# Chunk rows by broadcast copies, an early activation table, weights by need, and a first block in two 128-query parts

## The chip, the cores and the metric

One core of one Trainium2 chip. The metric is the device time of one execution in microseconds (us). One execution of each kernel is profiled: times inside a kernel come from its trace and count from the start of its span, which is about 2 us shorter than the timed run.

## The reference, cut to what matters

```python
# attention: 4 batches, 8 heads, 768 positions, head dim 64; chunks of 32 keys
k_min, k_max = min and max of every 32-key chunk
ub = sum_d max(q*k_min, q*k_max)                # upper bound of each chunk per query
ub = where(query chunk >= key chunk, ub, -1e9)
select the 6 chunks with the largest bound; mask the rest and the future
attn = softmax(q k^T / 8, masked) @ v
# FFN on the 3072 tokens of width 512
xn = x / rms(x) * rms_g
out = (silu(xn @ w_gate) * (xn @ w_val)) @ w_out   # d_ff 1536
```

A query among the first 192 has at most six chunks in its past, so it needs no bound: every past chunk is selected.

## The kernel before

The work is cut into 12 blocks of 256 queries (4 batches, 3 blocks each) and 24 jobs (a block and 4 of its 8 heads). For each job: k and q are loaded (`kraw`, `qraw`), transposed by VectorE (DVE) to `kT`, `qT`, cast to `kb`, `qb`; chunk minima and maxima go into `KS`; PE forms the bound `ub`; DVE turns and ranks it and makes a mask. Then scores `sc`, exponentials `pt`, values `avn`, normalised `xnat`. For each block follow `xs`, a turn by PE (`tp`), `xsT`, and the FFN: gate `gp`, value `vp`, hidden `hh`, output `op`.

The order of instructions on each engine is fixed in Python by a list scheduler: every operation has a planned duration, a priority (`key`, lower is sooner) and, for loads, a planned landing. An engine then works through its list in order; what stands at the head and waits holds everything behind it. Where PE's plan has a gap of over 0.5 us the kernel inserts matmuls on a zero tile ("idle matmuls"), meant to keep the clock up. Their number is fixed when the program is built; they run whether or not the gap is there on the chip.

```python
    warm(psF.tile([P, 512], FP32, name="wps", tag="bank")[:], 44)   # 44 idle matmuls first
    # ...
    def spread_rows(c0, c1, l0, l1, eng):      # the mask rows, from partitions 0-31 to the rest
        if eng == "SP":
            for a in range(1, 4):
                r = slice(32 * a, 32 * (a + 1))
                nc.sync.dma_start(out=late[r, l0:l1], in_=late[0:32, l0:l1])
                nc.sync.dma_start(out=chunkrow[r, c0:c1], in_=chunkrow[0:32, c0:c1])
            return
    # ...
    rows = add("SP", 2600.0, -3000.0, lambda e, w: spread_rows(BLK, S, BLK, S, "SP"), rows,
               lands=(300.0, 92.0))
    rm = add("SP", 430.0, SOON, lambda e, w: nc.sync.dma_start(
        out=rmsg[:], in_=moe_rms_g.rearrange("(g p) -> p g", p=P)), early=8000.0, lands=(100.0, 20.0))
    # ...
    key = blk_of(j) - 0.8 + 0.1 * g            # preparation of job j
    # ...
    key = blk + 3.1                            # FFN of block blk
```

The softmax here doesn't subtract the row's maximum and nothing guards it: scores larger than these inputs give would overflow.

## Time and profile before

Median 325.95 us.

| | us |
|---|---|
| span of the profiled execution | 324.1 |
| first real FFN matmul (gp) | 46.0 |
| PE idle plus idle matmuls before it | 32.1 |
| the same after it | 6.4 |
| k of job 4 reaches DVE | 29.9 |

The two rows of losses come from PE's timeline: I add the idle time in brackets, and for rows that read the zero tile the time until the next row begins. (The prediction's total, 37.2 us, leaves out the 1.25 us before the first matmul; it split that total as 31.5 and 5.7, where this count gives 32.1 and 6.4.) The page of the kernel before: busy time of each engine; then, in 40 slices of the span, the busy tenths of PE, its granted clock and the DMA engines' busy share.

```profile
PE 306.3 (95%) x4639; PEld 222.7 (69%) x4639; DVE 205.8 (64%) x525; ACT 225.0 (69%) x391; POOL 191.9 (59%) x332
...
PE   8977699989699999999999999999999999899995
...
PEclk9996999999799999999999999999999999999999
DMA  8999995465455442105453130100001001000001
```

PE looks full, but the first five slices (40 us) hold much that is not work. Its timeline (start us, duration us, what, and in brackets the idle time before and what ended it):

```profile
1.25 11.83 PE L263 MATMUL wps<-idle 128*128 128x512 bf16 x44 [1.25 <-DVE idle L258]
12.92 2.75 PE L263 MATMUL ub<-idle 128*128 128x512 bf16 x12
15.61 0.21 PE L421 MATMUL ub<-late,ident 64*64 64x32 bf16 x4
...
24.15 0.21 PE L421 MATMUL ub<-late,ident 64*64 64x128 bf16 x1 [1.19 <-DMA late<-late]
25.46 0.25 PE L421 MATMUL ub<-late,ident 64*64 64x128 bf16 x3 [1.10 <-DMA late<-late]
...
46.01 1.05 PE L649 MATMUL gp<-xsT,wg 128*128 128x256 bf16 x8
```

56 idle matmuls stand before the first bound at 15.6 us; PE then waits for spread rows; the FFN begins at 46 us. SyncE's timeline shows what stands before the loads of job 4:

```profile
15.80 0.40 SPq L751 DMA_DIRECT2D rmsg<-in_moe_rms_g_dram  x1
16.32 0.59 SPq L298 DMA_DIRECT2D late<-late  x1
...
20.60 4.54 SPq L233 DMA_DIRECT2D kraw<-in_k_dram  x4
```

The rms gain took 8.0 us to land, the rows about 7 us each.

### The profile page before, as it was taken

What the parts mean: (1) busy time and instruction counts of PE and PEld (TensorE: products, weight loads), DVE (VectorE), ACT (ScalarE), POOL (GpSimd) and SP (SyncE); (2) the same over time, 40 slices, a digit from 0 to 9 for tenths busy, and PEclk for the clock granted to TensorE, in tenths of its full rate; (3) what the DMA queues carried; (4) which work ended last, traced back from release to release, by engine and by line L of the source; (5) the groups of instructions that cost most, each with busy time, mean ns of one, the idle gap of its engine ahead of it and who ended that gap; (6) DMA issues with size and microseconds to landing.
All of it is one profiled execution on the core that took longest, in us unless ns stands there. A gap on an engine that the chain in (4) does not pass through costs nothing.

```text
span 324.1 us, 11419 instructions
## 1 busy us (share of the span) xinstructions
PE 306.3 (95%) x4639; PEld 222.7 (69%) x4639; DVE 205.8 (64%) x525; ACT 225.0 (69%) x391; POOL 191.9 (59%) x332
## 2 busy tenths in 40 slices
PE   8977699989699999999999999999999999899995
PEld 3434378658586787687685887785886876768682
DVE  7573989899499999159988577275466331523230
ACT  3251669786499998796778779766865986636461
POOL 8962538971896878297483567575452451635251
PEclk9996999999799999999999999999999999999999
DMA  8999995465455442105453130100001001000001
GB/s 170 203 213 237 225 164 145 123 167 163 137 144 132 145 121 68 67 2 132 132 136 96 51 85 16 53 2 35 34 3 37 31 3 67 0 34 32 34 32 66
DMA packets 43604, 30.30 MB, mean 93 GB/s; under 512 B 29536, under 2 KB 34336, under 8 KB 43552
## 3 DMA queue, kind: packets, MB, share of 16 engines
q1 hardware_dynamic: 34224, 23.81, 26.2%
q0 software_dynamic: 8944, 5.24, 11.4%
q8 instruction: 36, 0.59, 0.8%
q10 hardware_dynamic: 384, 0.52, 0.5%
q14 instruction: 16, 0.13, 0.1%
HBM read 28.31 MB, written 6.29 MB: 107 GB/s over the span
## 4 chain that ended last, share of the span: by engine, by line
PE 75%; DMA 8%; ACT 6%; DVE 5%; issue 2%; SPq 1%; POOL 1%; ACTq 0%; DVEq 0%; POOLq 0%
PE op L679 18%; PE gp L649 18%; PE vp L649 17%; PE avn L561 6%; DMA kraw<-in_k_dram 6%; PE sc L507 6%; PE ub L421 5%; ACT pt L531 3%; DMA rmsg<-in_moe_rms_g_dram 2%; PE sc L520 2%; PE tp L622 2%; SPq L233 1%; DVE kT L361 1%; ACT vs L661 1%; ACT th L657 1%
## 5 line engine op out<-in xcount | busy, mean ns | idle before, releaser
L672 POOL TENSOR_TENSOR hh<-tg,vs 128x512 bf16<-128x512 bf16 x72 | 83.5, 1160 | 54.2 <-ACT vs L661 44.9
L531 ACT ACTIVATE pt<-sc 128x768 bf16<-128x768 f32 (+1 forms) x96 | 84.1, 915 | 11.2 <-PE sc L520 10.9
L665 DVE SCALAR_TENSOR_TENSOR tg<-th,gp 128x512 bf16<-128x512 bf16 x72 | 49.0, 682 | 55.2 <-ACT th L657 53.8
L649 PE MATMUL vp<-xsT,wv 128*128 128x256 bf16 x576 | 75.4, 274 | 1.0 <-DVE tg L665 1.0
L649 PE MATMUL gp<-xsT,wg 128*128 128x256 bf16 x576 | 75.7, 275 | 0.0
L679 PE MATMUL op<-wo,hh 128*128 128x512 bf16 x288 | 65.2, 379 | 0.0
L649 PEld LDWEIGHTS <-wv 128*128 128x128 bf16 x576 | 54.8, 98 | 9.2 <-issue 1.5
L649 PEld LDWEIGHTS <-wg 128*128 128x128 bf16 x576 | 54.4, 98 | 8.4 <-issue 0.5
L661 ACT ACTIVATE vs<-vp 128x512 bf16<-128x512 f32 x72 | 43.3, 601 | 14.5 <-PE vp L649 10.8
L657 ACT ACTIVATE th<-gp 128x512 bf16<-128x512 f32 x72 | 43.3, 601 | 11.7 <-PE gp L649 11.6
L679 PEld LDWEIGHTS <-hh 128*128 128x128 bf16 x288 | 27.2, 98 | 30.7 <-POOL hh L672 0.3
L543 POOL TENSOR_SCALAR_AFFINE_SELECT pt<-pt 128x512 bf16<-128x512 bf16 x48 | 30.3, 643 | 23.9 <-ACT pt L531 23.1
L561 PE MATMUL avn<-VX,pt 128*128 128x65 bf16 x672 | 30.3, 195 | 5.3 <-POOL pt L543 2.8
L561 PEld LDWEIGHTS <-pt 128*128 128x128 bf16 x672 | 25.8, 98 | 11.1 <-POOL pt L543 3.1
L507 PE MATMUL sc<-qb,kb 32*128 32x256 bf16 (+1 forms) x768 | 32.4, 259 | 0.2 <-DVE ubn L431 0.2
L686 ACT ACTIVATE osb<-op 128x512 f32<-128x512 f32 x24 | 14.3, 597 | 24.8 <-PE op L679 24.8
L361 DVE STREAM_TRANSPOSE qT<-qraw 128x512 f32<-128x512 f32 x24 | 26.4, 1098 | 3.8 <-DMA qraw<-in_q_dram 3.7
L361 DVE STREAM_TRANSPOSE kT<-kraw 128x512 f32<-128x512 f32 x24 | 26.2, 1100 | 2.8 <-DMA kraw<-in_k_dram 2.7
L575 DVE RECIPROCAL rden<-avn 128x4 f32<-128x4 f32 x48 | 8.2, 172 | 26.1 <-PE avn L561 26.0
L520 PE MATMUL sc<-mt,chunkrow 32*128 32x128 bf16 (+1 forms) x352 | 23.8, 207 | 0.0
L520 PE MATMUL sc<-mo,chunkrow 32*128 32x128 bf16 (+1 forms) x352 | 22.8, 207 | 0.0
L592 ACT ACTIVATE junk<-xnat 128x512 bf16<-128x512 bf16 x24 | 15.2, 635 | 9.5 <-DVE xnat L582 9.1
(66 smaller groups left out, 384.1 us busy)
## 6 DMA issues: line engine op xcount, KB each, us to landing
out_dram<-osb SPq DMA_DIRECT2D x24, 256.0 KB, 2.1
kraw<-in_k_dram SPq DMA_DIRECT2D x92, 64.0 KB, 2.7
qraw<-in_q_dram SPq DMA_DIRECT2D x92, 64.0 KB, 2.3
vraw<-in_v_dram SPq DMA_DIRECT2D x40, 128.0 KB, 3.2
wg<-in_moe_w_gate_dram POOLq DMA_DIRECT2D x3, 512.0 KB, 10.1
wv<-in_moe_w_val_dram POOLq DMA_DIRECT2D x3, 512.0 KB, 12.5
wo<-in_moe_w_out_dram POOLq DMA_DIRECT2D x1, 1536.0 KB, 19.7
VX<-in_v_dram POOLq DMA_DIRECT2D x8, 64.0 KB, 5.7
```

What stands on the lines that cost most here:

```text
L361: nc.vector.transpose(out=st[j][nm + "T"].rearrange("p h (r j) -> p j h r", r=32, j=8), in_=st[j][nm + "raw"][:],)
L507: nc.tensor.matmul(sc[a // 2][:, a % 2, col:col + q1 - q0], st[jk]["kb"][r, t, ks], st[jq]["qb"][r, t, q0:q1], start=(t == 0), stop=(t == ...
L520: nc.tensor.matmul(sc[a // 2][:, a % 2, col + lo - q0:col + hi - q0], chunkrow[r, kr], mt[:, lo - m0 - C * w:hi - m0 - C * w], start=False ...
L531: nc.scalar.activation(out=u["pt"][:, hs, 0:W], in_=u["sc"][hp][:, :, 0:W], func=ACT.Exp, scale=SCALE)
L543: nc.gpsimd.affine_select(out=dg, in_=dg, compare_op=ALU.is_ge, fill=0.0, base=0, pattern=[[0, 2 * len(cols)], [1, P]], channel_multiplier=-1,
L561: nc.tensor.matmul(o[:, a, :], pt[:, a, off:off + P], vext[:, e, a, :], start=(kb == 0 and a == 0), stop=(kb == nkb - 1 and a == 3), skip_ ...
L649: nc.tensor.matmul(ps[:, i * W:(i + 1) * W], w[:, g, ht * P:(ht + 1) * P], xsT[c][:, g, 0:W], start=(g == 0), stop=(g == NP - 1), skip_gro ...
L657: nc.scalar.activation(out=th[:], in_=sl[c, hp, "gp"][:], func=ACT.Tanh, scale=0.5)
L661: nc.scalar.activation(out=vs[:], in_=sl[c, hp, "vp"][:], func=ACT.Copy, scale=0.5)
L665: nc.vector.scalar_tensor_tensor(out=tg[:], in0=sl[c, hp, "th"][:], scalar=1.0, in1=sl[c, hp, "gp"][:], op0=ALU.add, op1=ALU.mult,)
L672: nc.gpsimd.tensor_tensor(out=hh[:], in0=sl[c, hp, "tg"][:], in1=sl[c, hp, "vs"][:], op=ALU.mult)
L679: nc.tensor.matmul(op[:], sl[c, ht // K, "hh"][:, o:o + P], wo[:, ht, :], start=(ht == 0), stop=(ht == NHT - 1),)
```

## The change

Its intent: begin the FFN earlier and free SyncE's queue. The diff at its core (cut; whitespace and moved lines left out):

```diff
-    SPLIT = []
+    SPLIT = [blocks[0]]                       # first block: two 128-query parts, 128-token FFN pieces
@@ first loads
+        if j == min(3, 3):
+            nc.scalar.dma_start(out=rms_rows[:], in_=moe_rms_g.rearrange("(g p) -> g p", p=P))
-        load(j, "k", both if j < 2 else (nc.sync,))      # and q
+        load(j, "k", both if j < 3 else (nc.sync,))      # both = SyncE and ScalarE
+    nc.scalar.activation(out=first[:], in_=first[:], func=ACT.Exp)     # table early
-    warm(..., 44)
+    warm(..., 24)
@@ mask rows: fill_rows and spread_rows removed
+    for t, src in ((chunkrow, eye), (late, tri)):
+        nc.vector.tensor_copy(
+            t[:].rearrange("p (c t) -> p c t", t=CH),
+            src[:, 0:S // CH].unsqueeze(2).to_broadcast([P, S // CH, CH]))
@@ weights: planned times of the three thirds of gate and value, and of w_out
-            weights(nm, n, (7000.0, 12000.0, 17000.0, 22000.0)[n])
+            weights(nm, n, (6500.0, 8000.0, 10000.0, 15000.0)[n])
@@ rms gain: loaded as 4 rows, turned by PE, copied by DVE
+    rt = add("PE", 100.0, SOON, lambda e, w: turn_rms(), early=10000.0, take=(("F", 1),))
+    rm = add("DVE", 150.0, SOON, lambda e, w: nc.vector.tensor_copy(rmsg[:], rms_ps[0][:]), rt,
+             give=((rt, "F", 0),))
@@ priorities and planned latencies
-        key = blk_of(j) - 0.8 + 0.1 * g
+        key = blk_of(j) - 0.6 + 0.1 * g
-        key = blk + 3.1                       # FFN
+        key = blk + 2.5
-    ... d.seen + (200.0 if e == "PE" else 0.0)
+    ... d.seen + (400.0 if e == "PE" else 0.0)
     # also: values' key 0.0 -> -0.3, v loads planned 2.5 us longer,
     # xsT on ScalarE for two blocks instead of three, planned landings of the first loads
```

More of the change, by code (lines that the diff above doesn't have):

```diff
@@ L90, in ready @@
         for d in o.deps:
-            t = max(t, (d.end if e == "PE" else d.seen - 10.0) if d.eng == e else d.seen + (200.0 if e == "PE" else 0.0))
+            t = max(t, (d.end if e == "PE" else d.seen - 10.0) if d.eng == e else d.seen + (400.0 if e == "PE" else 0.0))
         return t
@@ L251 @@
     both = (nc.sync, nc.scalar)
+    rms_rows = const.tile([NP, P], FP32, name="rms_rows")
     for j in range(4):
-        load(j, "k", both if j < 2 else (nc.sync,))
-        load(j, "q", both if j < 2 else (nc.sync,))
+        if j == min(3, 3):
+            nc.scalar.dma_start(out=rms_rows[:], in_=moe_rms_g.rearrange("(g p) -> g p", p=P))
+        load(j, "k", both if j < 3 else (nc.sync,))
+        load(j, "q", both if j < 3 else (nc.sync,))
+    first = const.tile([P, 1], FP32, name="first")
+    nc.vector.memset(first[:], 0.0)
+    nc.scalar.activation(out=first[:], in_=first[:], func=ACT.Exp)
     idle = const.tile([P, 512], BF16, name="idle")
@@ L263, in warm @@
             nc.tensor.matmul(ps, idle[:, 0:P], idle[:], start=True, stop=True)
-    warm(psF.tile([P, 512], FP32, name="wps", tag="bank")[:], 44)
+    warm(psF.tile([P, 512], FP32, name="wps", tag="bank")[:], 24)
     chunkrow = const.tile([P, S], BF16, name="chunkrow")
@@ L275, in cast @@
             {"POOL": nc.gpsimd, "DVE": nc.vector}[eng].tensor_copy(out, in_)
-    def fill_rows(c0, c1, l0, l1):
-        cr, lt = chunkrow[0:32, c0:c1], late[0:32, l0:l1]
-        nc.gpsimd.memset(lt, NEG)
-        nc.gpsimd.affine_select(
-            out=lt, in_=lt, compare_op=ALU.is_ge, fill=0.0,
-            base=-1 - l0, pattern=[[-1, l1 - l0]], channel_multiplier=CH,
-        )
-        nc.gpsimd.memset(cr, MASKED)
-        nc.gpsimd.affine_select(
-            out=cr, in_=cr, compare_op=ALU.is_ge, fill=0.0,
-            base=c0, pattern=[[1, c1 - c0]], channel_multiplier=-CH,
-        )
-        nc.gpsimd.affine_select(
-            out=cr, in_=cr, compare_op=ALU.is_ge, fill=0.0,
-            base=CH - 1 - c0, pattern=[[-1, c1 - c0]], channel_multiplier=CH,
-        )
-    def spread_rows(c0, c1, l0, l1, eng):
-        if eng == "SP":
-            for a in range(1, 4):
-                r = slice(32 * a, 32 * (a + 1))
-                nc.sync.dma_start(out=late[r, l0:l1], in_=late[0:32, l0:l1])
-                nc.sync.dma_start(out=chunkrow[r, c0:c1], in_=chunkrow[0:32, c0:c1])
-            return
-        for a in range(1, 4):
-            r = slice(32 * a, 32 * (a + 1))
-            cast(eng, late[r, l0:l1], late[0:32, l0:l1])
-            cast(eng, chunkrow[r, c0:c1], chunkrow[0:32, c0:c1])
     ident = const.tile([P, P], BF16, name="ident")
     masks.make_identity(nc, ident[:])
+    eye = const.tile([P, CH], BF16, name="eye")
+    tri = const.tile([P, CH], BF16, name="tri")
+    nc.gpsimd.memset(tri[0:32, :], NEG)
+    nc.gpsimd.affine_select(
+        out=tri[0:32, :], in_=tri[0:32, :], compare_op=ALU.is_ge, fill=0.0,
+        base=-1, pattern=[[-1, CH]], channel_multiplier=1,
+    )
     own = const.tile([P, 2, CB], FP32, name="own")
@@ L312 @@
         nc.gpsimd.memset(own[32 * a:32 * (a + 1), a % 2, :], 1.0)
-    fill_rows(0, BLK, Q0, BLK)
+    eps6 = const.tile([P, 1], FP32, name="eps6")
+    nc.gpsimd.memset(eps6[:], 1.0e-6)
+    mhalf = const.tile([P, 1], FP32, name="mhalf")
+    nc.gpsimd.memset(mhalf[:], -0.5)
     KS = [persist.tile([P, 4, 2, CH], FP32, name=f"KS{i}") for i in range(2)]
     VX = [persist.tile([P, 2, 4, D + 1], BF16, name=f"VX{i}") for i in range(KEEP_K)]
+    for t in KS:
+        nc.gpsimd.memset(t[:], 0.0)
+    for t in VX:
+        nc.vector.memset(t[:, :, :, D:D + 1], 1.0)
+    for a in range(4):
+        r = slice(32 * a, 32 * (a + 1))
+        nc.vector.tensor_scalar(
+            out=eye[r, :], in0=ident[r, r], scalar1=MASKED, scalar2=None, op0=ALU.mult)
+        if a:
+            nc.vector.tensor_copy(tri[r, :], tri[0:32, :])
+    for t, src in ((chunkrow, eye), (late, tri)):
+        nc.vector.tensor_copy(
+            t[:].rearrange("p (c t) -> p c t", t=CH),
+            src[:, 0:S // CH].unsqueeze(2).to_broadcast([P, S // CH, CH]))
     def load_v_cast(j):
@@ L325, in load_v_cast, with turn_rms @@
                 in_=v[b, 4 * g:4 * g + 4, t0:t0 + P, :].rearrange("a p d -> p a d"))
-    for t in KS:
-        nc.vector.memset(t[:], 0.0)
-    for t in VX:
-        nc.vector.memset(t[:, :, :, D:D + 1], 1.0)
     for j in range(2):
         load_v_cast(j)
-    spread_rows(0, BLK, Q0, BLK, "DVE")
-    eps6 = const.tile([P, 1], FP32, name="eps6")
-    nc.gpsimd.memset(eps6[:], 1.0e-6)
-    mhalf = const.tile([P, 1], FP32, name="mhalf")
-    nc.gpsimd.memset(mhalf[:], -0.5)
-    rmsg = const.tile([P, NP], FP32, name="rmsg")
+    rmsg = const.tile([P, NP], FP32, name="rmsg")
+    ident4 = const.tile([NP, NP], FP32, name="ident4")
+    nc.vector.tensor_copy(ident4[:], ident[0:NP, 0:NP])
+    rms_ps = {}
+    def turn_rms():
+        rms_ps[0] = psF.tile([P, NP], FP32, name="rmsp", tag="bank")
+        nc.tensor.matmul(rms_ps[0][:], rms_rows[:], ident4[:], start=True, stop=True)
     ss_all = const.tile([P, NTOK // P], FP32, name="ss_all")
@@ L712 @@
     SOON = -1.0e6
-    T0 = {"k0": 5000.0, "q0": 5700.0, "k1": 6600.0, "q1": 7300.0, "v0": 8500.0, "v1": 9500.0,
+    T0 = {"k0": 4700.0, "q0": 5600.0, "k1": 5600.0, "q1": 6900.0, "v0": 8500.0, "v1": 9500.0,
           "k2": 10500.0, "q2": 11500.0, "k3": 12500.0, "q3": 13500.0}
@@ L745 @@
         for nm in ("wg", "wv"):
-            weights(nm, n, (7000.0, 12000.0, 17000.0, 22000.0)[n])
-    weights("wo", 0, (7000.0, 12000.0, 17000.0, 22000.0)[NW])
-    rows = add("POOL", 2600.0, 0.0, lambda e, w: fill_rows(BLK, S, BLK, S))
-    rows = add("SP", 2600.0, -3000.0, lambda e, w: spread_rows(BLK, S, BLK, S, "SP"), rows,
-               lands=(300.0, 92.0))
-    rm = add("SP", 430.0, SOON, lambda e, w: nc.sync.dma_start(
-        out=rmsg[:], in_=moe_rms_g.rearrange("(g p) -> p g", p=P)), early=8000.0, lands=(100.0, 20.0))
+            weights(nm, n, (6500.0, 8000.0, 10000.0, 15000.0)[n])
+    weights("wo", 0, (6500.0, 8000.0, 10000.0, 15000.0)[NW])
+    rt = add("PE", 100.0, SOON, lambda e, w: turn_rms(), early=10000.0, take=(("F", 1),))
+    rm = add("DVE", 150.0, SOON, lambda e, w: nc.vector.tensor_copy(rmsg[:], rms_ps[0][:]), rt,
+             give=((rt, "F", 0),))
     load_of = {}
@@ L757 @@
         if nm == "v":
-            o = add("SP", 860.0, -1000.0 + n, lambda e, w, j=j: load_v(j), lands=(1340.0, 20.0))
+            o = add("SP", 860.0, -1000.0 + n, lambda e, w, j=j: load_v(j), lands=(1340.0 + 2500.0, 20.0))
         else:
@@ L793 @@
         elif j < 4:
-            x["vc"] = add("POOL", 1650.0, SOON, lambda e, w, j=j: load_v_cast(j), early=8000.0,
+            x["vc"] = add("POOL", 1650.0, SOON, lambda e, w, j=j: load_v_cast(j), early=12000.0,
                           lands=(1920.0, 30.0))
         else:
-            x["vc"] = add(("POOL", "ACT"), 540.0, key + 0.0, lambda e, w, j=j: p_values(j, e), load_of["v", j])
-        if m:
-            x["ub"].deps.append(rows)
-            x["mt"].deps.append(rows)
+            x["vc"] = add(("POOL", "ACT"), 540.0, key + -0.3, lambda e, w, j=j: p_values(j, e), load_of["v", j])
     AVS = []
@@ L869 @@
             X["tp", tt] = f["tp"]
-        xt = add(("DVE", "ACT") if blk < 3 else "DVE", dict(DVE=570.0 * nt, ACT=1300.0), SOON,
+        xt = add(("DVE", "ACT") if blk < 2 else "DVE", dict(DVE=570.0 * nt, ACT=1300.0), SOON,
                  lambda e, w, c=c: keep_x(c, e), f["tp"], rm, give=((f["tp"], "F", 0),))
-        key = blk + 3.1
+        key = blk + 2.5
         for hp in range(NHT // K):
@@ L957 @@
     pe_free = 8500.0
-    free = {"PE": pe_free, "DVE": 5000.0, "ACT": 5800.0, "POOL": 7000.0, "SP": 11500.0}
+    free = {"PE": pe_free, "DVE": 4700.0, "ACT": 5800.0, "POOL": 6500.0, "SP": 11500.0}
     for o in arrange(ops, BANKS, free):
```

## The prediction

> **What bounds the kernel now.** TensorE's work plus a poor start. The busy table has PE at 95% (306.3 of 324.1 us), but part is matmuls on a zero tile that only keep the clock up. By the timeline PE loses 37.2 us: 12.6 idle and 24.6 in those idle matmuls, nearly all before 100 us (about 1 us after). The first real FFN matmul (gp) starts at 46.0 us, after only 14.5 us of real PE work: 31.5 us lost before it, 5.7 after it. The last 3.7 us are copy-out and store. So 283 us of real PE work are the floor.
>
> Why the start is slow (timeline, waits, DMA issues): 56 idle matmuls run to 15.6 us, although KS for the first bound was ready at 12.3. The q load of job 2 lands at 15.5. SyncE then issues the 2 KB rms gain, 8.0 us to landing, and six row spreads, about 7 us each; k of job 4 is issued from 20.6 and reaches DVE at 29.9 us. PE waits 2.3 us for late rows. DMA is saturated from 6 to 44 us; wo, issued at 24.0, lands 19.7 us later.
>
> **What the change does.**
> - The spreads and the rms load leave SyncE: 4.8 us ahead of job 4's loads. POOL loses five 0.5-0.6 us fills.
> - DVE gains seven 32-wide operations (about 0.1 us) and two 128x768 broadcast copies, about 0.9 us each (estimate from its 0.6 us 512-wide operations); six small copies go. kT of job 0 keeps its place near 4.5 us.
> - ACT issues 13 loads instead of 8. At the trace's 0.56 us each that ends at 8 us; only then come the 1.28 us table load and the first kb, about 9.6 us against 6.6. The skill ("ScalarE: Activation LUTs", What ACT_TABLE_LOAD costs) gives 1283 ns; the trace agrees. The early load is not hidden: it costs the start about 3 us, and DVE waits for the rms turn near 11-12 us.
> - Weights go out back to back from about 6.5 us, wo near 13.
> - The first 128 queries need no bound, so scores start near 10.5 us, and the first gp needs only 128 tokens. Following the per-engine order with the trace's durations I get it at 26 us (22 to 30), after about 6.5 us of real work.
> - 192 gate/value matmuls of 128 columns replace 96 of 256: 0.055-0.068 us each against 0.109: 0 to 2.5 us more.
> - Idle matmuls fall from 95 to 61.
>
> **On the critical path.** Loss before the first gp: 31.5 to 19.5 us. After it: 5.7 to 7-8, because block 0's FFN now shares 26-50 us with attention whose loads find DMA saturated. About 1 us of extra work; the 2.8 us POOL wait at 81-84 us and the half-rate stretch after it (gp 1.9 us instead of 1.04, granted clock 0.83; the skill, "TensorE: Matmul & The Clock Gate", Part 1, describes half rate after idleness) may go. Net: -11 us.
>
> **Time: 314.5 us, range 308 to 321.** Faster by over 2%: 0.83; within 2%: 0.15; slower: 0.02.
>
> **What would show it.** First gp near 26 us; no PE wait for late rows; k of job 4 on DVE before 25 us; wo landed before 35; first kb on ACT after 9; idle plus idle matmuls about 27 us; little change after 110 us.
>
> **What would make it wrong.** Weights starving the k/q loads (block 1's attention late); FFN consumed early (key 2.5) leaving too little to fill later waits; the rms turn holding DVE longer.

## The result, and the profile after

317.2 us median of 4 runs (316.54 to 317.55), the kernel before 325.37 us. The ratio is 0.9738, 95% interval 0.9692 to 0.9783: faster by 2.6%. Ratios here are the mean time of one kernel's fast runs over that of the kernel before in the same rounds, so not quite the ratio of the quoted medians. The page of the changed kernel:

```profile
PE 298.5 (94%) x4701; PEld 220.5 (70%) x4719; DVE 206.4 (65%) x532; ACT 225.5 (71%) x395; POOL 187.3 (59%) x328
...
PE   8497988989999999999999999999999999999994
...
PEclk9879999999999999999999999999999999999998
DMA  8999995466451546541026032001001000000001
```

PE's timeline:

```profile
12.48 0.29 PE L507 MATMUL sc<-qb,kb 32*128 32x128 bf16 x8 [3.16 <-ACT qb L279]
13.79 1.44 PE L269 MATMUL sc<-idle 128*128 128x512 bf16 x3 [1.01 <-ACT pt L531]
...
19.53 0.24 PE L421 MATMUL ub<-late,ident 64*64 64x32 bf16 x4
...
31.17 1.06 PE L649 MATMUL gp<-xsT,wg 128*128 128x128 bf16 x16
```

The FFN begins at 31.2 instead of 46.0 us and the waits for late rows are gone. The losses fall from 32.1 to 23.7 us before the first gp and rise from 6.4 to 7.0 us after it: 7.8 us in sum, for a span 8.3 us shorter. But the first bound is *later* than before (19.5 against 15.6 us). ScalarE's timeline says where that begins:

```profile
9.37 0.49 ACTq L255 DMA_DIRECT2D rms_rows<-in_moe_rms_g_dram  x1
9.90 1.28 ACT L262 ACT_TABLE_LOAD   x1 [9.90 <-DMA kraw<-in_k_dram]
...
11.30 0.61 ACT L279 ACTIVATE kb<-kT 128x512 bf16<-128x512 f32 x1
```

In the kernel before:

```profile
5.34 1.28 ACT L273 ACT_TABLE_LOAD   x1 [5.34 <-DMA kraw<-in_k_dram]
```

Thirteen load issues hold ScalarE until 9.9 us, so the "early" table load comes 4.6 us later than before, and the first cast at 11.3 instead of 6.6. DVE's timeline in the changed kernel shows the next wait:

```profile
10.19 0.68 DVE L373 TENSOR_REDUCE kmx<-kT 128x16 f32<-128x512 f32 x1
16.08 0.16 DVE L749 COPY rmsg<-rmsp 128x4 f32<-128x4 f32 x1 [5.21 <-PE rmsp L338]
16.16 0.67 DVE L373 TENSOR_REDUCE kmn<-kT 128x16 f32<-128x512 f32 x1
```

A copy of four columns stops DVE for 5.2 us; the second `KS` is ready at 17.5 us instead of 16.0. From there to 19.5 us PE is still in idle matmuls that stand ahead of the first bound, at a granted clock of 0.50. So two questions: what do these waits cost, and which part of the change paid?

### The profile page after: what moved, and what is told of

The parts are those of the page before. It is cut to its first block, busy times and chain, and to the rows that moved or that the text cites. A ratio compares the mean times of both kernels' runs of the same rounds, so it can differ in the third digit from the quotient of the medians.

```text
span 315.8 us, 11564 instructions
## 1 busy us (share of the span) xinstructions
PE 298.5 (94%) x4701; PEld 220.5 (70%) x4719; DVE 206.4 (65%) x532; ACT 225.5 (71%) x395; POOL 187.3 (59%) x328
## 4 chain that ended last, share of the span: by engine, by line
PE 69%; DMA 11%; DVE 8%; SPq 4%; issue 3%; ACT 2%; POOL 1%; ACTq 0%; DVEq 0%; POOLq 0%
PE gp L649 17%; PE vp L649 16%; PE op L679 16%; DMA qraw<-in_q_dram 9%; PE avn L561 5%; PE sc L507 5%; PE ub L421 5%; SPq L233 3%; DMA kraw<-in_k_dram 2%; PE sc L520 2%; DVE kT L361 2%; PE tp L622 2%; DVE qT L361 1%; DVE kmx L373 1%; DVE kmn L373 1%
## 5 line engine op out<-in xcount | busy, mean ns | idle before, releaser
L531 ACT ACTIVATE pt<-sc 128x1024 bf16<-128x1024 f32 (+3 forms) x100 | 84.2, 885 | 11.5 <-PE sc L520 9.6
L649 PE MATMUL gp<-xsT,wg 128*128 128x256 bf16 (+1 forms) x624 | 75.2, 265 | 1.1 <-issue 0.7
L649 PE MATMUL vp<-xsT,wv 128*128 128x256 bf16 (+1 forms) x624 | 74.8, 264 | 0.2 <-DVE tg L665 0.2
L679 PE MATMUL op<-wo,hh 128*128 128x512 bf16 x275 | 64.3, 379 | 0.8 <-issue 0.2
L649 PEld LDWEIGHTS <-wv 128*128 128x128 bf16 x624 | 55.5, 98 | 7.5 <-issue 0.8
L543 POOL TENSOR_SCALAR_AFFINE_SELECT pt<-pt 128x512 bf16<-128x512 bf16 (+1 forms) x52 | 30.8, 609 | 17.5 <-ACT pt L531 16.9
L507 PE MATMUL sc<-qb,kb 32*128 32x256 bf16 (+1 forms) x784 | 33.2, 255 | 4.0 <-ACT qb L279 3.2
L507 PEld LDWEIGHTS <-kb 32*128 32x128 bf16 x784 | 13.8, 92 | 15.0 <-issue 10.6
L582 DVE TENSOR_TENSOR xnat<-avn,rden 128x256 bf16<-128x256 f32 x48 | 20.4, 424 | 1.8
## 6 DMA issues: line engine op xcount, KB each, us to landing
wo<-in_moe_w_out_dram POOLq DMA_DIRECT2D x1, 1536.0 KB, 27.9
```

The lines of the kernel that those rows point to most:

```text
L507: nc.tensor.matmul(sc[a // 2][:, a % 2, col:col + q1 - q0], st[jk]["kb"][r, t, ks], st[jq]["qb"][r, t, q0:q1], start=(t == 0), stop=(t == ...
L531: nc.scalar.activation(out=u["pt"][:, hs, 0:W], in_=u["sc"][hp][:, :, 0:W], func=ACT.Exp, scale=SCALE)
L543: nc.gpsimd.affine_select(out=dg, in_=dg, compare_op=ALU.is_ge, fill=0.0, base=0, pattern=[[0, 2 * len(cols)], [1, P]], channel_multiplier=-1,
L649: nc.tensor.matmul(ps[:, i * W:(i + 1) * W], w[:, g, ht * P:(ht + 1) * P], xsT[c][:, g, 0:W], start=(g == 0), stop=(g == NP - 1), skip_gro ...
L679: nc.tensor.matmul(op[:], sl[c, ht // K, "hh"][:, o:o + P], wo[:, ht, :], start=(ht == 0), stop=(ht == NHT - 1),)
```

## The experiments

All gave correct results. Each was timed in five rounds against the kernel before. Their runs are compared by their ratios; a difference of two ratios carries about 0.006 of uncertainty (estimate: the two half-widths combined). The two losses are taken from PE's timeline as above.

| run | median us | ratio to before (95%) | first gp us | loss before / after it, us |
|---|---|---|---|---|
| changed kernel | 317.2 | 0.9738 (0.9692-0.9783) | 31.2 | 23.7 / 7.0 |
| act_two | 318.11 | 0.9771 (0.9734-0.9807) | 32.1 | 23.4 / 6.1 |
| rms_late | 317.36 | 0.9738 (0.9704-0.9772) | 30.2 | 22.5 / 7.9 |
| act_two_rms_late | 316.62 | 0.9722 (0.9687-0.9757) | 30.7 | 21.9 / 6.1 |
| no_split | 321.09 | 0.9856 (0.9819-0.9892) | 46.0 | 31.7 / 6.2 |
| rows_only | 322.14 | 0.9910 (0.9863-0.9958) | 42.9 | 29.9 / 5.5 |
| keys_old | 323.21 | 0.9931 (0.9890-0.9973) | 30.5 | 22.6 / 13.3 |
| weights_old | 318.81 | 0.9796 (0.9755-0.9836) | 30.4 | 25.0 / 7.2 |
| land_true | 313.72 | 0.9635 (0.9592-0.9678) | 24.2 | 18.4 / 8.3 |
| ffn_key_old | 319.42 | 0.9817 (0.9781-0.9852) | 31.4 | 24.1 / 8.7 |
| no_split_keys_old | 323.37 | 0.9949 (0.9907-0.9992) | 43.3 | 29.5 / 7.0 |
| land_act3 | 315.8 | 0.9705 (0.9669-0.9741) | 29.4 | 23.5 / 7.0 |
| land_more | 329.38 | 1.0110 (1.0066-1.0153) | 24.4 | 18.1 / 21.2 |

### What holds the start

**act_two**: the order on PE, DVE and POOL is unchanged by this edit.

```diff
-            nc.scalar.dma_start(out=rms_rows[:], ...)
+            nc.sync.dma_start(out=rms_rows[:], ...)
-        load(j, "k", both if j < 3 else (nc.sync,))     # and q
+        load(j, "k", both if j < 2 else (nc.sync,))
```

> The changed kernel, but ScalarE issues loads of jobs 0 and 1 only (8 instead of 13 issues); job 2 and the rms rows are issued by SyncE alone. Orders of PE, DVE and POOL stay the same. Theory A (ScalarE's 13 issues hold back its table load, its casts, and through the rms turn DVE for 5.2 us): table load at about 5.4 us instead of 9.9, first kb at 6.7 instead of 11.3, DVE's wait for the rms turn under 1 us, first gp near 27 us instead of 31.2, time 3 us (1%) below the changed kernel's 317.2. Theory B (the saturated DMA sets the start): the casts come earlier but the loads of jobs 2 to 4 land later, the first gp moves by under 1 us and the time stays within 1 us.

The table load came at 5.3 and the first kb at 6.7 us, as expected, but nothing was won: 318.11 us. DVE still waited 5.3 us for the rms turn, because the rms rows, now behind job 2's loads on SyncE, became the next holder of PE. PE's waits in the first 32 us of this run (us in total, times, longest):

```profile
PE rmsp L338 <- DMA rms_rows<-in_moe_rms_g_dram: 4.3, 1, 4.3
```

So the run does not separate the theories: it took one wait away and put another in the same place.

**rms_late** moves only the planned time of the turn.

```diff
-    rt = add("PE", 100.0, SOON, lambda e, w: turn_rms(), early=10000.0, ...)
+    rt = add("PE", 100.0, SOON, lambda e, w: turn_rms(), early=15000.0, ...)
```

> The changed kernel with the turn of the rms gain planned at 15 us instead of 10 us: PE does it after the second bound, DVE copies it after the first bound's maxima, so that DVE's second kmn no longer waits for it. Theory A (DVE's 5.2 us wait for the rms turn delays the second KS and the first bound behind it): DVE goes on at 10.9 us, the second KS is ready near 12 instead of 17.5 us, the first bound at about 17.7 instead of 19.5, first gp near 29, time about 2 us lower. Theory B (PE waits for ScalarE's casts and for DMA anyway): first gp and time within 0.7 us of the changed kernel.

DVE's wait for the turn vanished and the second `KS` was ready at 13.8 instead of 17.5 us, but the first bound stayed at 19.7 and the time at ratio 0.9738. That is theory B's outcome in time; the first gp came 1.0 us earlier, a little more than B allowed. What stood before the bound is on PE's own list. PE waited 3.8 us for the cast `qb` and started at 12.6; the granted clock was then 0.50 until 19.3, and eight idle matmuls ran ahead of a bound whose inputs were ready:

```profile
16.16 2.72 PE L269 MATMUL ub<-idle 128*128 128x512 bf16 x6 [0.47 <-ACT pt L531]
19.11 0.71 PE L269 MATMUL ub<-idle 128*128 128x512 bf16 x2 [0.22 <-issue]
19.74 0.21 PE L421 MATMUL ub<-late,ident 64*64 64x32 bf16 x4
```

No run takes these idle matmuls out, so what they cost is not shown. Meanwhile DVE waited 4.6 us for k loads in the first 32 us.

**act_two_rms_late** does both.

> Both edits together. Theory A: since the first edit alone already takes nearly all of DVE's wait away, both together are worth little more than the first edit, 3 to 4 us under the changed kernel, first gp near 26 us. Theory B: no more than 1 us in all.

Now the first bound is at 14.2 us, 5.3 us earlier than in the changed kernel, yet the first gp moves by only 0.5 us and the ratio by 0.0016, within the intervals. Theory A, as I wrote it, falls: the two waits are not enough. DVE's timeline in this run shows the third holder:

```profile
16.69 0.63 DVE L373 TENSOR_REDUCE kmx<-kT 128x16 f32<-128x512 f32 x1
19.36 1.10 DVE L361 STREAM_TRANSPOSE kT<-kraw 128x512 f32<-128x512 f32 x1 [2.04 <-DMA kraw<-in_k_dram]
20.31 0.20 DVE L431 STREAM_TRANSPOSE ubn<-ub 128x64 f32<-128x64 f32 x1
...
23.19 0.42 DVE L582 TENSOR_TENSOR xnat<-avn,rden 128x256 bf16<-128x256 f32 x1
```

The bound is ready at about 15 us and the first `avn` at 17, but DVE stands before the transpose of job 3's k, which lands at 19.3 us; the scheduler had planned it for 12.5. The first piece needs none of job 3.

**land_true** adds the landings that the trace shows to the previous edit.

```diff
-    T0 = {..., "k1": 5600.0, "q1": 6900.0, ..., "k2": 10500.0, "q2": 11500.0, "k3": 12500.0, "q3": 13500.0}
+    T0 = {..., "k1": 6700.0, "q1": 8500.0, ..., "k2": 13000.0, "q2": 16000.0, "k3": 19500.0, "q3": 22000.0}
```

> As act_two_rms_late, with the planned landings of the first loads set to what the trace shows (k of job 2 at 13, q 16, k of job 3 at 19.5, q 22 us), so that DVE does the first 128 queries' ranks and normalise before it stands waiting for job 3's k. Theory D (DVE's in-order queue, blocked behind loads of jobs 2 and 3 that the saturated DMA delivers late, holds the first piece): first gp near 25 us instead of 30.7, time 3 us under act_two_rms_late, 313.5. Rival (what is won early is lost to weights landing at 23 to 33 us or to block 1's attention, which waits for the same loads): first gp earlier but time within 1 us.

First gp at 24.2 us, 313.72 us, ratio 0.9635 against 0.9722: theory D's outcome. The size is from runs on two chips, each with its own runs of the kernel before. The edit redraws the whole plan (POOL's order and the number of idle matmuls change too), so that DVE's order did it is read from the trace. DVE's timeline, with the normalise now ahead of job 3's transpose:

```profile
17.91 0.42 DVE L582 TENSOR_TENSOR xnat<-avn,rden 128x256 bf16<-128x256 f32 x1
...
19.48 1.06 DVE L361 STREAM_TRANSPOSE kT<-kraw 128x512 f32<-128x512 f32 x1
```

The transpose loses nothing by standing later: it starts 0.1 us after its start in the run above. This version beats both kernels of the study.

**land_act3** puts ScalarE's 13 issues back into land_true (the first edit undone, the other two kept).

> land_true with ScalarE's 13 load issues put back (rms rows on ScalarE again). With DVE no longer blocked, ScalarE's late first cast (11.4 instead of 6.4 us) should now show: first gp 2 to 4 us later than land_true's 24.2 and time 2 to 3 us higher, 316. Rival (the casts have slack, as act_two on the changed kernel suggests): time within 0.8 us of land_true's 313.7.

Ratio 0.9705 against 0.9635, 315.8 us, first gp at 29.4 us (5.2 later, more than expected). PE's longest wait in the first 32 us:

```profile
PE sc L507 <- ACT qb L279: 5.3, 1, 5.3
```

So ScalarE's issues do cost about 2 us, but only once DVE no longer hides them. The reverse holds too. With rms_late these runs are four corners, all with the late turn; ratio, and first gp in us:

| | landings as first planned | landings as traced |
|---|---|---|
| 13 issues on ScalarE | 0.9738, 30.2 | 0.9705, 29.4 |
| 8 issues | 0.9722, 30.7 | 0.9635, 24.2 |

Either edit alone moves the first gp by under 1 us and the ratio by nothing clear of noise; both together bring it 6.0 us forward, for 0.0103 of ratio. Two holders stood side by side, and by the first gp each hid the other.

### Which part of the change paid

**no_split**

```diff
-    SPLIT = [blocks[0]]
+    SPLIT = []
```

> The changed kernel without the split of the first block (256 queries and 256-token FFN pieces throughout). If the split is what brings the FFN forward: first gp near 37 us, time about 4 us higher, 321. If the gain came from the freed SyncE queue and the early weights alone: under 1 us higher, first gp later but PE kept busy by block 1's attention.

321.09 us, 0.0118 of ratio above the changed kernel: taking the split out costs about 3.8 us (0.0118 of 325), as theory one had it, though the first gp was at 46.0, not 37. In this run PE also stood 7.1 us waiting for the rms rows to land; with the turn planned later it might not have, so how much of the 3.8 us is that wait is open. In the losses the split saves more, 7.2 us (37.9 against 30.7). About 1.4 us of the difference are its narrower matmuls: 16 of 128 columns took 0.99 us, 0.062 each, and 192 of them replace 96 of 0.109 (estimate from these). The remaining 1.4% against the kernel before does not show in the losses (37.9 against 38.4 us in all). Part of it is the clock: in the kernel before it was 0.83 between 80 and 90 us, after a 2.5 us wait for POOL, and full there without that wait; over the whole profiled execution its mean was 0.983 against 0.989, at most 0.6% or 2 us (estimate). The rest I could not attribute.

**rows_only** is the kernel before with the row copies, the rms rows and turn, and nothing else of the change.

```diff
 # against the changed kernel
-    SPLIT = [blocks[0]] ; both if j < 3 ; early Exp ; warm 24 ; new weights, keys and landings
+    SPLIT = []          ; both if j < 2 ; no Exp    ; warm 44 ; old weights, keys and landings
-    rt = add(... early=10000.0 ...)
+    rt = add(... early=15000.0 ...)
```

> The kernel before with one part of the change alone: chunk and late rows by broadcast copies and the rms gain turned by PE (planned at 15 us), so the six spreads and the element-wise rms load leave SyncE's queue. No split, weights, keys, opening matmuls and ScalarE's loads as before. Theory R (this part is what remains of the gain without the split, about 4.4 us of 8): time near 321.5 us, k of job 4 on DVE near 24 us instead of 29.9. Rival (the rest comes from keys and weights): gain under 1.5 us, 324 to 325.5, even if job 4's k comes earlier.

Ratio 0.991, 0.9% (about 3 us), between the two expectations. k of job 4 reached DVE at 25.9 us against 29.9, and PE's waits for late rows were gone.

**keys_old** puts back the priorities and the planned latencies together.

```diff
-        key = blk_of(j) - 0.6 + 0.1 * g
+        key = blk_of(j) - 0.8 + 0.1 * g
-        key = blk + 2.5
+        key = blk + 3.1
-    ... 400.0 if e == "PE" ...          # and v loads +2500, values' key -0.3, xsT blk < 2
+    ... 200.0 if e == "PE" ...          # v loads as planned before, key 0.0, blk < 3
```

> The changed kernel with the old priorities (FFN 3.1 blocks later instead of 2.5, preparation 0.8 blocks ahead instead of 0.6, values at 0.0, ScalarE takes xsT for three blocks, 200 ns across engines instead of 400, v loads planned as short). Theory K (the priorities carry part of the gain): 1.5 to 2.5 us slower than the changed kernel, with new PE waits between 45 and 110 us. Rival (the gain is at the start, before the priorities matter): within 0.8 us, first gp still near 31 us.

323.21 us: 6 us slower than the changed kernel, far more than I expected, with the first gp even a little earlier (30.5 us). All is lost after it: 13.3 us against 7.0. PE's waits between 45 and 110 us, first in keys_old:

```profile
PE avn L561 <- POOL pt L543: 1.8, 2, 1.4
PE sc L269 <- ACT pt L531: 1.7, 1, 1.7
PE tp L622 <- ACT xs L607: 1.4, 2, 1.2
PE avn L561 <- DVE xnat L582: 0.8, 1, 0.8
PE tp L622 <- DVE xs L610: 0.8, 1, 0.8
```

and in the changed kernel:

```profile
PE sc L269 <- ACT pt L531: 1.3, 2, 1.1
PE sc L520 <- issue: 0.7, 1, 0.7
PE ub L269 <- ACT pt L531: 0.3, 1, 0.3
```

**ffn_key_old** puts back only `key = blk + 3.1`.

> The changed kernel with only the FFN's priority put back (3.1 blocks later instead of 2.5). Theory F (of the priorities this one matters: with 3.1 the ready FFN stands behind attention that is waiting, so PE idles between 45 and 110 us): most of the 6 us of keys_old, 321 to 323, with about 10 us idle or in idle matmuls after the first gp. Rival (the loss of keys_old comes from the preparation's lead and the planned latencies): within 1.5 us of the changed kernel, up to 318.7.

Ratio 0.9817, 0.0079 of the 0.0193 that keys_old costs: the FFN's priority is not most of it, nor nothing. The rest lies in the other parts of keys_old (the preparation's lead, the values' key, the engine of `xsT`, the planned latencies) or in how they act together; they were not tried apart.

**no_split_keys_old** is the fourth corner (no_split and keys_old together).

> The changed kernel without the split and with the old priorities: the fourth corner beside the changed kernel (317.2), no_split (321.1) and keys_old (323.2). If the two parts add up independently (split 4, priorities 6): 327. If the priorities are worth their 6 us only where the split has put FFN work into the start: 321 to 322.5, like rows_only.

323.37 us. The four corners as ratios to the kernel before:

| | old priorities | new priorities |
|---|---|---|
| whole block | 0.9949 | 0.9856 |
| split | 0.9931 | 0.9738 |

With old priorities the split is worth 0.0018, nothing clear of the intervals; with new ones 0.0118. The priorities are worth 0.0093 alone and 0.0193 with the split. ("Priorities" includes the planned latencies, as in keys_old.) The two parts pay 0.0100 more together than apart; that is just clear of noise, about 0.008 here (estimate: the four half-widths combined). My reading: the split brings FFN work forward (gp from 43.3 to 30.5 us), the priorities decide whether it fills PE's waits, as the two lists of waits under keys_old show. My second expectation (321 to 322.5) was the nearer one, but the priorities are not worthless without the split.

**weights_old**

```diff
-            weights(nm, n, (6500.0, 8000.0, 10000.0, 15000.0)[n])
+            weights(nm, n, (7000.0, 12000.0, 17000.0, 22000.0)[n])     # w_out and the v loads of jobs 2 and 3 likewise
```

> The changed kernel with the weights issued at the old times (7, 12, 17, 22 us). Theory W (early weights are needed by the earlier FFN): PE waits for wg or wv between 31 and 45 us, time 2 us higher. Rival (early weights only take bandwidth from the loads of jobs 2 and 3, which DVE waits for): job 3's k is transposed earlier than 21.6 us or at the same time, no PE wait for weights, time equal or up to 1.5 us lower.

Ratio 0.9796 against 0.9738, near 2 us slower but with intervals that overlap, and neither reason is seen: PE waited for no weight, and job 3's k came to DVE later (24.8 against 21.6 us), not earlier. The schedule was drawn anew; POOL issued w_out at 29.1 us ahead of work for job 3, whose `KS` was ready at 31.7 instead of 25.3 us. Inconclusive about the weights themselves.

**land_more** tries to go on from land_true.

```diff
-    weights("wo", 0, (6500.0, 8000.0, 10000.0, 15000.0)[NW])
+    weights("wo", 0, 20000.0)
-            o = add("SP", 1720.0, ..., lands=(740.0, 92.0))            # k and q loads of jobs 4 on
+            o = add("SP", 1720.0, ..., lands=(740.0 + 1500.0, 92.0))
```

> land_true with the remaining loads planned 1.5 us longer and wo planned at 20 instead of 15 us, since DVE still waits 2.9 us for q of job 4 at 28 us (PE 2.1 us behind it) and POOL 1.3 us to issue wo. If the same rule (plan landings as the trace has them) goes on paying: DVE's wait for job 4's q under 1 us, time 1 to 2 us below land_true, 312 to 313. Rival (the remaining loss is spread over ScalarE's exponentials and the schedule only reshuffles): within 1 us, either sign.

A clear miss: 329.38 us, slower than the kernel before. The start is kept (first gp 24.4 us; DVE's wait for a q load falls from 2.9 to 0.9 us), but the losses after it rise from 8.3 to 21.2 us, 11.9 of them after 110 us. The 1.5 us were not measured landings but a guess for 20 jobs alike; which of them spoiled the later plan, or whether wo's later issue did, was not looked into. Traced landings helped, a blanket margin hurt.

## Why the prediction was right or wrong

The predicted 314.5 us (308 to 321) holds the measured 317.2, and a gain of 11 us was forecast where 8.2 were measured. Point by point:

- **PE's start bounds the kernel, and the change works there: right.** The loss before the first gp fell by 8.4 us (32.1 to 23.7); after 110 us there is 0.2 us of idle time against 1.0, too little to matter.
- **First gp at 26 us (22 to 30): mis-sized, 31.2.** The failing term is "Loss before the first gp: 31.5 to 19.5": 23.7 was measured. The sum followed each engine's order, but with waits that were too short or missing. I had seen that DVE would wait for the rms turn "near 11-12 us" and took it for short; it lasted until 16.1. The k of job 3, at which DVE stands once the first two waits are gone, was not in it, nor the half clock from 13.6 to 20.4 us.
- **"The early load ... costs the start about 3 us": the delay was right, its cost was wrong here.** First kb at 11.3 us (9.6 predicted). But act_two and act_two_rms_late remove it for no clear gain, since another wait takes its place: for the rms rows in act_two, for job 3's k in act_two_rms_late. In land_act3 it costs 0.007 of ratio, about 2 us.
- **k of job 4 on DVE before 25 us: missed, 26.8**, though 3.1 us earlier than before. **w_out landed before 35 us: wrong.** It was issued at 17.8 us, took 27.9 us and landed at 45.7, later than before (24.0 + 19.7 = 43.7): with the DMA engines 90% busy or more from 8 to 47 us in both kernels, the earlier issue did not bring it in sooner. The first op was at 55.8 us, so it cost nothing that the waits show.
- **Loss after the first gp from 5.7 to 7-8 us: right as a number (6.4 to 7.0), for a reason that I had not given.** I named the FFN's priority of 2.5 only as a risk. With the old priorities this loss is 13.3 us and the split's gain is gone. A term of several us was missing from the argument, so it was partly luck that this number came out right.
- **Half rate after idleness: right at the place named, missed at another.** The wait for POOL at 81-84 us and the slow clock behind it are gone. But a new one came: the changed kernel idles 3.2 us before 12.5 us, and its granted clock is 0.50 from 13.6 to 20.4 us; three idle matmuls at 13.8 us take 1.44 us, where six took 1.47 us at 20.5. "TensorE: Matmul & The Clock Gate", Part 1, of the Trainium skill describes such a half rate after idleness.

## What to carry to other kernels

With in-order engines, look at what stands at the *head* of each list during a stall, and plan a load where the trace says it lands: here removing ScalarE's visible wait paid nothing clear of noise until two transposes were also moved behind work that did not need them, and the other way round. A wait that can be removed at no gain may have a second one beside it. Filler work such as idle matmuls holds what stands behind it too, so look for it ahead of ready work. Work brought forward by the split paid little here without the priorities that let it fill waits, so test such parts in all four combinations. And a compute engine that issues loads first comes late to its own work: 13 issues instead of 8 moved ScalarE's first instruction from 5.3 to 9.9 us.

## What the Trainium skill lacked or had wrong

- "DMA: Bandwidth & Descriptors", Issuing engines are not separate DMA queues: it says that issuing from several engines only saves the sequencer's time, "usually small relative to the DMA itself". The runs agree: k of job 2 reached DVE at 12.6 us with two issuers (rms_late) and 12.8 with one (act_two_rms_late), q, which the single issuer took until 10.6 instead of 8.8 us to issue, at 13.9 and 15.7; and one issue of about 0.5 us is small beside some 2.5 us to landing. What it lacks is the case of an issuer that also computes: 13 issues held ScalarE from 0.8 to 9.9 us.
- "TensorE: Matmul & The Clock Gate", Part 1: it gives about 3.4 us of sustained work to return to full rate. After the wait for POOL in the kernel before, the granted clock stood at 0.50 for about 3.4 us (84.2 to 87.6), which agrees. In the changed kernel it stood there for about 6.8 us (13.6 to 20.4), though PE had almost unbroken work from 13.8 us. The page calls its window free-running, so two windows would fit; that was not tested.
- "ScalarE: Activation LUTs", What ACT_TABLE_LOAD costs: the 1283 ns agree with the trace (1.28 us). The further drain of about 1380 ns, which it gives for a switch to a different set, does not follow this load: the next activation starts 1.29 us after the load's start (9.90 to 11.19 us). This is ScalarE's first instruction and no switch between sets, so the page is not contradicted; it lacks this case.
- No page that I read has the cost of issuing weights early into a full DMA: w_out's time to landing grew from 19.7 to 27.9 us when it was issued 6.2 us sooner.
